# Agent attention with soft MoE: round weights in the selection matrices, denominators from slot sums, no filler products, a new order

## The chip, the cores and the metric

The kernel runs on one core of a Trainium2 chip. The core has TensorE (PE, matrix products into PSUM), VectorE (DVE), ScalarE (ACT), GpSimd (POOL) and SyncE (SP, which issues the large transfers); 16 DMA engines move data. The metric is the device time of one execution in microseconds; the median of several runs counts.

## The reference

Attention through 49 agents per batch, then a soft mixture of experts over all 4 x 11456 rows. All data is float32.

```python
B, N, C = 4, 11456, 128            # q, k, v; agents: (4, 49, 128)
def sm(a, b):                       # softmax(scale * a @ b^T)
    s = scale * (a @ b.transpose(0, 2, 1)); s = s - s.max(-1, keepdims=True)
    e = np.exp(s); return e / (e.sum(-1, keepdims=True) + 1e-09)
agent_v = sm(agents, k) @ v         # (B, 49, 128)
x = (sm(q, agents) @ agent_v).reshape(B * N, C)
# soft MoE: 8 experts, 4 slots each, so 32 slots; phi: (128, 32)
logits = x @ phi
d = np.exp(logits - logits.max(0)); d /= d.sum(0) + 1e-09     # over all rows, for each slot
slot_input = (d.T @ x).reshape(8, 4, 128)
slot_out[e] = np.maximum(slot_input[e] @ w1[e], 0) @ w2[e]    # F = 1024
c = np.exp(logits - logits.max(1)); c /= c.sum(1) + 1e-09     # over the slots, for each row
out = c @ slot_out
```

## The kernel before

The rows of a batch are laid out as four streams of 90 cells with 32 rows each. They are loaded in groups of 16 cells (1024 KB; the last groups of a batch are smaller): 24 K groups, 24 V groups and 25 q groups.

- A **K group**: `kx` and `kv` load it, `ks` makes the agent scores on PE, `km`, `kz`, `kb`, `kr` keep the running maximum, `ke` takes the exponential on ACT, `kT` transposes on DVE, `kE` (line 315, `ev`) multiplies with V on PE and `kA` adds to the batch's accumulator on DVE. After a batch's last group `kg` and `kh` make `agent_v` and `bd_m`, agents times `phi`.
- A **q group**: `qx` loads, `qs` scores, `qt` transposes on DVE so that a row's 49 scores lie side by side, `qm` takes the maximum. In the even groups (`DEN_ACT`) ACT takes the exponential with its sum (`qE`); in the odd ones POOL subtracts (`qu`), ACT takes the exponential (`qe`) and DVE sums 49 columns (`qd`, line 445). `qw`, `qr`, `qN` divide; `qp` and `qc` transpose on PE and copy on ACT.
- A **round** is two q groups (the last is the seventh group of batch 3 alone); there are 13. `ql` makes the slot logits on PE in PSUM (`lq`), `qM`, `r2`, `r4`, `r3` find each slot's maximum (`m_all`), `qv` transposes the logits into `x_all` on DVE, where they stay for the output. `r5` turns the maximum into a row (`mb`), `ru` subtracts it on POOL (line 546), `re` takes the exponential on ACT (line 551), and `rg` multiplies with the agent weights into `gp` (line 559); `rc` copies that to `g_all`. `cr`, `cu`, `ce` prepare the output's softmax in place in `x_all`.
- The **tail**: the rounds' maxima give each round a weight (`nm`, `wt`, `wr`, `ws`). The weights of the first nine rounds (batches 0 to 2) are made ahead (`ea` to `ei`), those of the last four at the end. POOL scales `g_all` by the weights (`ee`, `gl`), PE sums the rounds with the matrix `sel_st` (`ef`, `gm`, `l1`) and makes the slots' inputs `si` (`l3`, `l4`). `d0` to `d2` make the denominators from `g_all`'s last column. Then `mh` (`hp`, line 753), `mr` (relu, `hs`), `mt` (`htp`), `mc` (`ht`), `mo` (`so_p`, line 785) are the experts, `ms`, `sb`, `sd` spread and scale their outputs into `sob`. `fl` are filler products that nobody reads.
- The **output**, in 25 chunks of `x_all`: `os`, `oe`, `or`, `om` normalise, `ot` transposes on DVE, `oo` multiplies with `sob` on PE, `va` (DVE) and `vb` (ACT) copy PSUM to SBUF, `od` stores.

All steps stand in one list, `ORDER`, written out as a table of tokens. Every engine, and SP's queue of transfers, works through its own steps in that order, each waiting for its inputs; nothing overtakes. A buffer (`BUFS`) goes to the next taker in the list's order. w1 and w2 come in eight loads of 1024 KB: three of w2 take q buffers, the others take the room of the K and V buffers and so wait for the last K group (`ends`).

```python
FILL = (3, 2, 2, 2)
CHUNKS = [4, 4, 8] + [16] * 21 + [8]
    ends = [(f, i) + x for i in range(NK - 3, NK) for f, x in (
        ("ks", (1,)), ("ke", (1,)), ("kT", ()), ("kE", ()))]
```

Of the kernel before, what the change touches and what calls it, by code (L numbers as in the profile page):

```python
# [50 lines left out]
ORDER = """
qx5 wu qs5.0 qs5.1 qt5 qm5 qx0 qs0.0 qs0.1 qt0 qx3 qu5 qe5 qm0 qs3.0 qE0.0 qd5 qw5 qs3.1 qt3 qm3
qE0.1 qE0.2 qE0.3 qw0 qu3 qe3 qx2 qs2.0 qs2.1 qt2 qm2 qE2.0 kx0 ks0.0 ks0.1 qr5 km0 kz0 qd3 qx1
qs1.0 qs1.1 qx4 kb0 kr0 qE2.1 ke0.0 qN5 qs4.0 qs4.1 qr0 qt1 qw3 qN0 kp0 kx1 qm1 qt4 qr3 qm4 ks1.0
qE2.2 ks1.1 qp0.0 qp0.1 ke0.1 kT0 qN3 qE2.3 qE4.0 km1 kz1 qx6 qs6.0 qs6.1 kb1 kr1 qw2 qr2 qc0 qt6
qu1 qe1 kx2 ke1.0 ke1.1 qE4.1 ka1 ks2.0 ks2.1 qd1 km2 qN2 qp2.0 qp2.1 qx7 kT1 qw1 qr1 qN1 kp1 qc2
kz2 qE4.2 qE4.3 qs7.0 qs7.1 kx3 qt7 kv0 kb2 kr2 qp3.0 qp3.1 qc3 qw4 qm7 qu7 ke2.0 ke2.1 qm6 qE6.0
qr4 qx8 qN4 ks3.0 ks3.1 km3 ka2 kE0 qp1.0 kA0 kz3 qs8.0 qs8.1 kp2 kb3 qp1.1 kT2 qe7 qE6.1 qd7 kr3
qw7 qc1 qE6.2 qE6.3 qr7 ke3.0 qw6 kv1 kE1 kx5 ks5.0 ks5.1 qN7 kA1 qt8 qm8 ke3.1 kp3 ka3 kT3 kx4
qE8.0 qE8.1 ks4.0 qr6 ks4.1 km4 kz4 kv2 kE2 kb4 kr4 kp4 ke4.0 km5 ke4.1 kz5 kx6 ks6.0 ks6.1 kA2  # L60
qE8.2 kT4 kb5 kr5 qE8.3 ka4 ke5.0 qw8 qN6 ke5.1 kv3 kE3 km6 kz6 kb6 kr6 kT5 kv4 qr8 qN8 kE4 ke6.0
kA3 kA4 ka5 kv5 kE5 qx11 qs11.0 qs11.1 ke6.1 cx0 kA5 kg5.1 kT6 kg5.2 kh5.1 kg5.3 kh5.2 kh5.3 ql1
qt11 qm11 qx9 qp4.0 qM1 qv1 kh5.4 qu11 qe11 qd11 r21 qp4.1 qc4 qs9.0 qs9.1 qt9 ql0 qM0 r20 qw11
qr11 qN11 kx8 qp6.0 r41 qp6.1 qc6 kx7 ks7.0 r31 qv0 ks7.1 km7 qp5.0 r40 kp6 r30 qp5.1 kz7 qc5 r50
ru0.0 ks8.0 ks8.1 qm9 kb7 kr7 qx12 ke7.0 ke7.1 qs12.0 qs12.1 ql2 kp7 re0.0 rg0.0 km8 kz8 qt12
ru0.1 re0.1 r51 qm12 rg0.1 kb8 rc0 qx10 qs10.0 qM2 kr8 r22 qu9 qv2 ru1.0 ru1.1 qe9 qE12.0 ka8
qs10.1 qt10 qE12.1 kp8 kv6 r42 r32 kx9 qd9 kT7 kE6 kA6 ks9.0 ks9.1 km9 qm10 qp8.0 qp8.1 kz9 qE12.2
qE12.3 qw12 kv7 kE7 qr12 cr3 ke8.0 qN12 qc8 ke8.1 ka7 kA7 kT8 kb9 re1.0 kr9 qE10.0 re1.1 kp9 kx10
ks10.0 qw9 ke9.0 cr4 ks10.1 rg1.0 qx13 km10 qs13.0 qs13.1 ke9.1 kz10 rg1.1 kb10 kx11 ks11.0 ks11.1
kT9 qE10.1 qE10.2 kr10 rc1 ke10.0 kv8 kx12 qr9 kE8 qt13 qN9 km11 kz11 kp10 kb11 qm13 kr11 kA8 qu13  # L70
qz5 ke10.1 ka10 r52 ru2.1 ru2.0 qe13 ka11 re2.1 cu3 ks12.0 kT10 ks12.1 km12 kz12 ke11.0 ka9 ke11.1
kv9 kE9 cr0 kb12 kr12 kA9 cr1 cu1 kT11 qd13 qp7.0 kv10 kE10 qE10.3 ke12.0 qw10 qr10 cr2 kA10 kv11
ke12.1 kp12 qN10 kE11 qp7.1 qw13 qc7 kA11 kg11.1 kg11.2 kh11.2 kT12 qr13 cr5 qN13 cu2 qx15 qs15.0
qs15.1 qt15 re2.0 kh11.4 kh11.1 qm15 qu15 kg11.3 kh11.3 rg2.0 rg2.1 rc2 ql3 kx13 qM3 r23 qp10.0
qp10.1 qc10 qv3 qe15 qd15 ce2 ks13.0 ks13.1 km13 qw15 r43 r33 r53 qp11.0 qp11.1 kz13 qc11 qx14
# [955 lines left out]
```

## Time and profile before

| what | value |
|---|---|
| median of 3 runs | 293.61 us (293.21 to 293.80) |
| the profiled execution | 293.71 us, span 291.9 us |
| busy share of the span: PE, DVE, ACT, POOL | 85%, 76%, 68%, 44% |
| read from memory, written | 79.98 MB, 23.59 MB |
| end of the last K group's products (`kE`) | 189.0 us |
| start of the experts' first product (`hp`) | 215.6 us |
| issue of the first output transfer | 231.9 us |

The span runs from the first to the last instruction; the execution's own time is 1.8 us longer. The three times at the foot cut the span into the loads with their work, the tail and the output.

### The profile page before, as it was taken

The numbers are of one execution on the slowest core, as the hardware profiler recorded it, in microseconds if no ns is written. First come the engines' busy times: TensorE is split into PE (matmuls) and PEld (weight loads), VectorE is DVE, ScalarE is ACT, GpSimd is POOL, SyncE is SP. The second block draws the span as 40 slices with busy tenths as digits, with TensorE's granted clock in tenths as the row PEclk, the third lists the DMA queues.
The fourth block names the chain that finished last, engine by engine and source line by source line (L and its number), as shares of the span: only waits on it lengthen the run. The fifth ranks groups of instructions, "written<-read, shape, count | busy, mean of one in ns | idle before, by whom it ended". The sixth has DMA issues, their size and how long they took to land.

```text
span 291.9 us, 8505 instructions
## 1 busy us (share of the span) xinstructions
PE 249.5 (85%) x3382; PEld 134.1 (46%) x3382; DVE 222.3 (76%) x431; ACT 199.6 (68%) x678; POOL 128.9 (44%) x135
## 2 busy tenths in 40 slices
...
GB/s 276 384 423 419 419 422 356 417 420 418 423 320 355 425 419 337 416 371 392 419 391 382 423 390 352 96 360 424 368 7 0 44 408 424 413 421 423 412 422 274
DMA packets 16311, 104.12 MB, mean 357 GB/s; under 512 B 1936, under 2 KB 2192, under 8 KB 5008
## 3 DMA queue, kind: packets, MB, share of 16 engines
...
q14 instruction: 12, 0.10, 0.1%
HBM read 79.98 MB, written 23.59 MB: 355 GB/s over the span
## 4 chain that ended last, share of the span: by engine, by line
PE 53%; DMA 32%; DVE 5%; ACT 4%; issue 2%; SPq 1%; POOL 1%; ACTq 0%; DVEq 0%
DMA out<-ot 12%; PE sk L238 10%; PE ev L315 10%; PE sq L238 9%; PE tp L466 7%; DMA kt<-kT 7%; DMA vt<-vL 7%; DMA qt<-qT 6%; PE lq L514 4%; PE gp L559 3%; ACT ot L841 3%; PE fl L850 1%; PE so_p L785 1%; PE hp L753 1%; DVE ct L820 1%
## 5 line engine op out<-in xcount | busy, mean ns | idle before, releaser
L455 POOL TENSOR_TENSOR pt<-pt,rt 128x784 f32<-128x784 f32 (+3 forms) x20 | 27.1, 1356 | 55.9 <-DVE rt L451 37.6
L238 PE MATMUL sk<-kt,ag 128*32 128x512 f32 (+1 forms) x384 | 46.2, 570 | 3.4 <-DMA kt<-kT 2.6
L238 PE MATMUL sq<-qt,ag 128*32 128x512 f32 (+3 forms) x400 | 44.4, 562 | 4.8 <-DMA qt<-qT 4.8
L440 ACT ACTIVATE pt<-pt,mx 128x49 f32<-128x49 f32 x148 | 47.5, 325 | 0.0
L315 PE MATMUL ev<-vt,et 128*64 128x129 f32 x720 | 44.6, 275 | 2.9 <-DMA vt<-vL 1.8
L841 ACT COPY ot<-pb 128x1536 f32<-128x1536 f32 (+2 forms) x25 | 32.5, 1311 | 16.9 <-DMA out<-ot 12.3
L315 PEld LDWEIGHTS ev<-vt,et 128*64 128x64 f32 x720 | 39.4, 136 | 9.3 <-issue 3.4
L828 PE MATMUL pa<-ct,sob 32*128 32x512 f32 (+2 forms) x50 | 32.4, 759 | 11.8 <-DVE ct L820 9.3
L546 POOL TENSOR_TENSOR dt<-x_all,mb 128x512 f32<-128x512 f32 (+3 forms) x25 | 29.2, 1189 | 19.8 <-DVE mb L542 9.4
L298 ACT ACTIVATE es<-sk,nm 128x512 f32<-128x512 f32 (+1 forms) x48 | 30.0, 650 | 10.1 <-DVE nm L289 4.6
L828 PE MATMUL pb<-ct,sob 32*128 32x512 f32 (+2 forms) x150 | 33.1, 760 | 0.0
L814 POOL TENSOR_TENSOR x_all<-x_all,cd 128x512 f32<-128x512 f32 (+2 forms) x25 | 23.4, 963 | 20.2 <-DVE cd L809 20.2
L471 ACT COPY pT<-tp 128x1024 f32<-128x1024 f32 (+3 forms) x25 | 23.1, 923 | 10.1 <-PE tp L466 9.9
L838 DVE COPY ot<-pa 128x512 f32<-128x512 f32 (+2 forms) x25 | 15.4, 620 | 18.6 <-DMA out<-ot 15.7
L270 DVE TENSOR_REDUCE mt<-sk 128x2 f32<-128x1024 f32 (+1 forms) x24 | 27.7, 1154 | 2.3 <-PE sk L238 2.1
L308 DVE STREAM_TRANSPOSE et<-es 128x1024 f32<-128x1024 f32 (+1 forms) x24 | 28.0, 1165 | 0.5 <-ACT es L298 0.4
L440 ACT ACTIVATION_READ_ACCUMULATOR pt<-pt,mx 128x1 f32 x148 | 27.9, 188 | 0.0
L415 DVE STREAM_TRANSPOSE pt<-sq 128x1024 f32<-128x1024 f32 (+3 forms) x20 | 21.8, 1095 | 7.6 <-PE sq L238 7.4
L571 POOL TENSOR_TENSOR x_all<-x_all,r_all 128x512 f32<-128x512 f32 (+3 forms) x25 | 23.7, 968 | 4.9 <-DVE r_all L567 3.5
L828 PEld LDWEIGHTS pa<-ct,sob 32*128 32x128 f32 x50 | 9.7, 230 | 33.1 <-DVE ct L820 19.8
L238 PEld LDWEIGHTS sq<-qt,ag 128*32 128x32 f32 x400 | 11.2, 111 | 24.8 <-issue 19.6
L425 POOL TENSOR_TENSOR pt<-pt,mx 128x784 f32<-128x784 f32 (+2 forms) x10 | 12.9, 1290 | 20.0 <-DVE mx L420 15.4
(120 smaller groups left out, 433.5 us busy)
## 6 DMA issues: line engine op xcount, KB each, us to landing
...
vt<-vL SPq DMA_DIRECT2D x20, 1032.0 KB, 10.2
qt<-qT SPq DMA_DIRECT2D x20, 1024.0 KB, 10.0
...
```

The lines of the kernel that those rows point to most:

```text
L238: t_.matmul(sp[32 * q4:32 * q4 + 32, h, :nt], ag[:, b, 32 * h:32 * h + 32], xv[:, q4, :], start=True, stop=True)
L270: v_.tensor_reduce(out=k["mt"][:, 0:2], in_=k["s"][:, :, :nt], axis=AX.X, op=ALU.max, negate=True)
L298: s_.activation(out=k["e"][:, h, :nt], in_=k["s"][:, h, :nt], func=AF.Exp, bias=k["nm"][:, 2 * h:2 * h + 1])
L308: v_.transpose(out=k["et"][:, :n].rearrange("p t (h a) -> p h t a", h=2), in_=k["e"][:, :, :nt].rearrange("p h (t a) -> p h t a", a=32))
L315: t_.matmul(k["ev"][o:o + AW, :], k["et"][:, c, :], k["v"][:, c, :], start=c < 2, stop=c >= n - 2)
L440: s_.activation(out=x, in_=x, func=AF.Exp, bias=q["mx"][:, c:c + 1], accum_out=q["rt"][:, c:c + 1])
L455: g_.tensor_tensor(out=x, in0=x, op=ALU.mult, in1=q["rt"][:, :n].unsqueeze(2).to_broadcast([P, n, A]))
L546: g_.tensor_tensor(out=q["dt"][:, :q["n"]], in0=x_all[:, q["at"]:q["at"] + q["n"]], op=ALU.subtract, in1=r["mb"].unsqueeze(1).to_broadcast ...
L571: g_.tensor_tensor(out=x_all[:, x], in0=x_all[:, x], op=ALU.subtract, in1=r_all[:, x].unsqueeze(2).to_broadcast([P, q["n"], S]))
L814: g_.tensor_tensor(out=x, in0=x, op=ALU.mult, in1=z["cd", j].unsqueeze(2).to_broadcast([P, n, S]))
L828: t_.matmul(pb[:, r - 1, :32 * n] if r else pa[:, :32 * n], sob[32 * r:32 * r + 32, :], z["ct", j][32 * r:32 * r + 32, :32 * n], start=Tru ...
L841: s_.copy(out=o_ov(j)[:, 1:4], in_=z["pb", j][:, :, :32 * CHUNKS[j]])
```

## The change

- **Constants and first loads.** The five 128-column matrices after `CO_AB` are gone; `sel_st` and `sel_ts` are cut from `sel_d`, `sel_on` is set on the chip. The first load of the agents brings batch 0's alone, the others come with `cx` and are scaled in a new step `am`.
- **Folds.** In the q groups 5, 9, 13, 17, 21 POOL adds the two halves of 50 columns (`qf`), and DVE sums 25 columns.
- **Late rounds.** `m_all` holds the negative maximum. In the rounds 10, 11 and 12 ACT takes the exponential straight from PSUM with the maximum as its bias (`rx`), and DVE transposes that into `dt` (`ry`); `r5`, `ru` and `re` are gone there.
- **Round weights.** `ws` multiplies the weights into the selection matrix (`wse`), so that PE's sum scales; the steps `ee`, `gl` on POOL and `l0` on DVE are gone, and the last round is copied by `rc` as the others.
- **Denominators.** They come from the last row of the rounds' sums `gt` by small products (`dE`, `d1`, `d3`).
- **Experts.** `si` is written with a stride of 36 and read with one of 32, so that the eight experts' outputs land in the rows of their slots and add up in one PSUM tile: one `ms`, one `sb`. `sd` moves from ACT to DVE. `hp` of the first four experts comes first.
- **No `fl`; chunks** `[4, 4, 8, 8] + [16] * 21`; **all of `ORDER` is new**.

```diff
 ORDER = """
-qx5 wu qs5.0 qs5.1 qt5 qm5 qx0 qs0.0 qs0.1 qt0 qx3 qu5 qe5 qm0 qs3.0 qE0.0 qd5 qw5 qs3.1 qt3 qm3
+wu qx0 qs0.0 qs0.1 kx0 ks0.0 ks0.1 qt0 qm0 qx1 qs1.0 qE0.0 qE0.1 qE0.2 km0 qs1.1 qt1 qx5 qE0.3 qm1
...
-FILL = (3, 2, 2, 2)
+FILL = (0, 0, 0, 0)
+LATE_EXP = (10, 11, 12)
+FOLD = (5, 9, 13, 17, 21)
 WARM = 5
-CHUNKS = [4, 4, 8] + [16] * 21 + [8]
+CHUNKS = [4, 4, 8, 8] + [16] * 21
...
+        def qf():
+            q["fo"] = rp.tile([P, QC, A1 // 2], F32, name=f"fo_{i}", tag="fo", bufs=2)
+            g_.tensor_tensor(out=q["fo"][:, :n], in0=q["pt"][:, :n, 0:A1 // 2],
+                             in1=q["pt"][:, :n, A1 // 2:A1], op=ALU.add)
...
+        def rx():
+            r["dT"] = tile_("pt", [P, 2, QC, 32], f"dT_{ri}")
+            s_.activation(out=r["dT"][:, :, :n // 2], in_=r["lp"][:, :, :n // 2], func=AF.Exp,
+                          bias=m_all[:, ri:ri + 1])
+
+        def ry(q):
+            q["dt"] = tile_("dt", [P, QC, S], f"dt_{q['i']}")
+            c, m = q["c0"] // 2, q["n"] // 2
+            v_.transpose(out=q["dt"][:, :2 * m].rearrange("p (j e) s -> p e j s", e=2),
+                         in_=r["dT"][:, :, c:c + m])
...
     def z_ws(e):
-        lo, hi = (0, n0) if e else (n0, NR + 1)
-        v_.tensor_copy(out=wrs[:, lo:hi], in_=z["wr", e])
+        lo, hi = (0, n0) if e else (n0, NR)
+        sh = [P, hi - lo, S]
+        v_.tensor_tensor(out=wse[:, lo:hi], op=ALU.mult,
+                         in0=z["wr", e][:, :hi - lo].unsqueeze(2).to_broadcast(sh),
+                         in1=sel_st.unsqueeze(1).to_broadcast(sh))
...
-            t_.matmul(out_, g_all[:, ri, :], sel_st, start=ri == R0[b],
+            t_.matmul(out_, g_all[:, ri, :], wse[:, ri, :], start=ri == R0[b],
...
-    def gscale(lo, hi):
-        g_.tensor_tensor(out=g_all[:, lo:hi], in0=g_all[:, lo:hi], op=ALU.mult,
-                         in1=wrs[:, lo:hi].unsqueeze(2).to_broadcast([P, hi - lo, A1]))
+    def dsum(out_, bs):
+        for b in bs:
+            t_.matmul(out_, gt[:, b, :], ident[0:A1, A:A1], start=b == bs[0], stop=b == bs[-1])
...
-    def z_d0():
-        v_.tensor_reduce(out=gs1[:, 0:1], in_=g_all[:, n0:NR, A], axis=AX.X, op=ALU.add)
-        v_.scalar_tensor_tensor(out=gs1[:, 0:1], in0=gs1[:, 1:2], scalar=wrs[:, NR:NR + 1],
-                                in1=gs1[:, 0:1], op0=ALU.mult, op1=ALU.add)
```

**SP's queue, from batch 0's fourth K load to its last V load.** `kt`, `vt` and `qt` are loads of K, V and q. Ahead of these rows stand eight q and three K loads in before:

```order
L232 DMA kt_400<-kT 128x2048
L261 DMA vt_404<-vL 128x2064
L232 DMA qt_437<-qT 128x2048
L261 DMA vt_522<-vL 128x2064
L232 DMA kt_541<-kT 128x1280
L232 DMA kt_564<-kT 128x2048
L261 DMA vt_588<-vL 128x2064
L232 DMA kt_620<-kT 128x2048
L261 DMA vt_656<-vL 128x2064
L261 DMA vt_686<-vL 128x2064
L261 DMA vt_714<-vL 128x1290
```

and five q, four K and one V load in the change:

```order
L230 DMA qt_374<-qT 128x2048
L259 DMA vt_402<-vL 128x2064
L230 DMA kt_429<-kT 128x2048
L230 DMA kt_455<-kT 128x1280
L259 DMA vt_489<-vL 128x2064
L637 DMA cs<-cst 128x224
L638 DMA ph<-phi 128x32
L639 DMA ag<-agT 128x192
L259 DMA vt_521<-vL 128x2064
L230 DMA qt_567<-qT 128x2048
L259 DMA vt_586<-vL 128x2064
L259 DMA vt_605<-vL 128x1290
```

Two q loads (`qx7`, `qx8`) and batch 1's first K load (`kx6`) moved behind the last V load of batch 0; the constants moved ahead of it.

**DVE's queue, the end of round 11.** `t` and `m_all` are its maximum, `mb` the row made of it, `dt` and `dT` its exponentials, `cd` sums and reciprocals for the output, `r_all` row maxima. Before, from the last maximum to the last round's scaling `l0`:

```order
L538 TENSOR_REDUCE m_all<-t_2987 128x1
L657 TENSOR_REDUCE nmx<-m_all 32x1
L802 TENSOR_REDUCE cd_3007<-x_all 128x16
L525 STREAM_TRANSPOSE x_all<-lq_2903 128x2x11x32
L542 STREAM_TRANSPOSE mb_3051<-m_all 128x32
L802 TENSOR_REDUCE cd_3060<-x_all 128x16
L674 COPY wrs<-wr_3058 128x5
L567 TENSOR_REDUCE r_all<-x_all 128x16
L802 TENSOR_REDUCE cd_3085<-x_all 128x16
L809 RECIPROCAL cd_2753<-cd_2753 128x16
L719 TENSOR_SCALAR g_all<-gp_3066,wrs 128x50
```

In the change, from the last maximum to `l2`'s copy of the sums:

```order
L545 TENSOR_REDUCE m_all<-t_3020 128x1
L687 TENSOR_REDUCE nmx<-m_all 32x1
L838 TENSOR_REDUCE cd_3030<-x_all 128x16
L738 COPY de<-de_p 32x1
L565 STREAM_TRANSPOSE dt_3078<-dT_3036 128x2x8x32
L565 STREAM_TRANSPOSE dt_3080<-dT_3036 128x2x3x32
L845 RECIPROCAL cd_2816<-cd_2816 128x16
L704 TENSOR_TENSOR wse<-wr_3083,cs 128x128
L565 STREAM_TRANSPOSE dt_3111<-dT_3007 128x2x2x32
L532 STREAM_TRANSPOSE x_all<-lq_2843 128x2x16x32
L758 COPY gt<-gt_p 50x32
```

The transposes into `dt` and the product `wse` are new on DVE; the transpose of round 10's logits into `x_all` moved behind them.

**DVE's queue, from `si` to the second relu** (`hs`). Before:

```order
L733 TENSOR_TENSOR si<-si_p,sie 128x8x4
L567 TENSOR_REDUCE r_all<-x_all 128x6
L802 TENSOR_REDUCE cd_3170<-x_all 128x16
L567 TENSOR_REDUCE r_all<-x_all 128x16
L760 TENSOR_SCALAR hs_3177<-hp_3156 128x512
L567 TENSOR_REDUCE r_all<-x_all 128x16
L737 TENSOR_REDUCE gs_106<-g_all 128x1
L738 SCALAR_TENSOR_TENSOR gs_106<-gs_106,wrs 128x1
L760 TENSOR_SCALAR hs_3195<-hp_3180 128x512
```

In the change:

```order
L765 TENSOR_TENSOR si<-si_p,sie 128x8x4
L838 TENSOR_REDUCE cd_3141<-x_all 128x16
L532 STREAM_TRANSPOSE x_all<-lq_3009 128x2x11x32
L838 TENSOR_REDUCE cd_3147<-x_all 128x16
L797 TENSOR_SCALAR hs_3159<-hp_3150 128x512
L585 TENSOR_REDUCE r_all<-x_all 128x16
L797 TENSOR_SCALAR hs_3173<-hp_3164 128x512
```

The two steps on `gs` between the relus are gone, and round 11's transpose into `x_all` stands ahead of the first.

## Rows read from the trace of the kernel before

**Rows 1.** The page: busy time, granted clock, and rate of the DMA in 40 slices.

```profile
PE 249.5 (85%) x3382; PEld 134.1 (46%) x3382; DVE 222.3 (76%) x431; ACT 199.6 (68%) x678; POOL 128.9 (44%) x135
...
GB/s 276 384 423 419 419 422 356 417 420 418 423 320 355 425 419 337 416 371 392 419 391 382 423 390 352 96 360 424 368 7 0 44 408 424 413 421 423 412 422 274
```

**Rows 2.** Windows: stretch, length, busy us of each engine, clock, DMA share, GB/s.

```profile
0.00:10.00 10.00, 8.10 (x42) 4.21 (x42) 1.85 (x8) 1.70 (x2) 0.74 (x5) 1.00 0.80 310
10.00:31.00 21.00, 17.09 (x152) 5.66 (x152) 17.89 (x24) 17.70 (x85) 8.49 (x8) 1.00 1.01 411
31.00:70.00 39.00, 34.73 (x442) 19.92 (x434) 29.87 (x50) 28.00 (x123) 11.02 (x12) 1.00 1.00 407
70.00:189.00 119.00, 115.66 (x1945) 66.33 (x1944) 108.24 (x197) 96.10 (x374) 64.20 (x63) 1.00 0.94 373
189.00:203.20 14.20, 13.47 (x285) 9.60 (x284) 12.93 (x38) 11.06 (x27) 10.32 (x12) 1.00 0.90 370
203.20:215.50 12.30, 9.48 (x142) 6.61 (x139) 6.84 (x22) 4.56 (x15) 5.58 (x8) 0.58 0.63 259
215.50:231.90 16.40, 14.14 (x214) 8.82 (x215) 12.45 (x31) 7.33 (x23) 12.35 (x15) 0.90 0.01 2
231.90:245.00 13.10, 8.35 (x60) 2.76 (x55) 10.80 (x28) 9.43 (x14) 5.99 (x7) 0.92 0.95 386
245.00:291.90 46.90, 28.48 (x128) 10.24 (x120) 21.39 (x40) 23.77 (x21) 10.16 (x11) 0.68 0.96 396
```

**Rows 3.** The chain that ended last: start, length, engine and step, 184 to 229 us.

```profile
184.98 1.02 PE tp L466 x8
186.00 3.02 PE ev L315 x52
...
203.25 2.50 issue
...
215.57 3.57 PE hp L753 x16
...
222.25 2.00 PE htp L769 x16
...
224.91 3.75 PE so_p L785 x128
```

**Rows 4.** Timeline of PE, the start.

```profile
1.20 4.63 PE L618 MATMUL wu<-si 128*128 128x256 f32 x10 [1.20 <-DVE si L195]
```

**Rows 5.** Groups of instructions by shape: busy us, mean ns, idle before them.

```profile
L445 DVE TENSOR_REDUCE rt<-pt 128x16 f32<-128x784 f32 x6 | 5.7, 942 | 0.3 <-ACT pt L430 0.2
L445 DVE TENSOR_REDUCE rt<-pt 128x10 f32<-128x490 f32 x3 | 1.9, 639 | 0.0
L820 DVE STREAM_TRANSPOSE ct<-x_all 128x512 f32<-128x512 f32 x21 | 13.8, 681 | 0.3 <-POOL x_all L814 0.3
L298 ACT ACTIVATE es<-sk,nm 128x512 f32<-128x512 f32 x40 | 26.1, 677 | 8.3 <-DVE nm L289 4.6 <-DVE et L308 2.8 <-DVE rt L451 1.0
L551 ACT ACTIVATE dt<-dt 128x512 f32<-128x512 f32 x20 | 12.2, 626 | 0.7 <-POOL dt L546 0.5
L546 POOL TENSOR_TENSOR dt<-x_all,mb 128x512 f32<-128x512 f32 x20 | 25.7, 1300 | 16.1 <-DVE mb L542 9.4 <-PE sq L238 3.7 <-ACT pT L471 2.2
L546 POOL TENSOR_TENSOR dt<-x_all,mb 128x320 f32<-128x320 f32 x3 | 2.6, 881 | 0.1
```

**Rows 6.** Timeline of DVE, 220 to 224 us.

```profile
220.55 1.04 DVE L738 SCALAR_TENSOR_TENSOR gs<-gs,wrs 128x1 f32<-128x1 f32 x1
221.52 0.68 DVE L760 TENSOR_SCALAR hs<-hp 128x512 f32<-128x512 f32 x1
222.12 1.26 DVE L802 TENSOR_REDUCE cd<-x_all 128x16 f32<-128x512 f32 x2
```

**Rows 7.** SyncE: when it issues the first output, and a row of its waits.

```profile
231.87 4.42 SPq L845 DMA_DIRECT2D out<-ot  x5
...
SPq L261 <- PE ev L315: 12.4, 3, 7.6
```

More of the change, by code (lines that the diff above doesn't have):

```diff
@@ L56 @@
[L56 to L73, printed above, removed]
@@ L480, in q_ops @@
         x = o("qx", (), "D", qx, takes=("qt",))
-        s0 = o("qs", (0,), "P", lambda: qs_(0), deps=(x,), takes=("s",), gives=(("qt", x),))
+        s0 = o("qs", (0,), "P", lambda: qs_(0), deps=(x, ("am", 0)) if b else (x,), takes=("s",), gives=(("qt", x),))
         s1 = o("qs", (1,), "P", lambda: qs_(1), deps=(x, s0), gives=(("qt", x),))
@@ L592, in r_ops @@
         f = o("r3", (), "V", r3, deps=(f,), gives=(("a", qM_),))
-        mb = o("r5", (), "V", r5, deps=(f,))
+        late = ri in LATE_EXP
+        if late:
+            mb = o("rx", (), "A", rx, deps=(f, l0), takes=("pt",), gives=(("s", l0),))
+            ops[v]["deps"].append(mb)
+        else:
+            mb = o("r5", (), "V", r5, deps=(f,))
         g0 = None
@@ L606, in r_ops, with am @@
             g0 = g0 or f
-        if ri < NR - 1:
-            o("rc", (), "A", rc, deps=(f,), gives=(("a", g0),))
-        r["end"], r["g0"] = f, g0
+        r["end"] = o("rc", (), "A", rc, deps=(f,), gives=(("a", g0),))
     def cx():
-        nc.sync.dma_start(out=cs[:, CO_AB:], in_=cst[:, CO_AB:])
+        nc.sync.dma_start(out=cs[:, CO_1:], in_=cst[:, CO_1:])
         nc.sync.dma_start(out=ph, in_=phi)
+        nc.sync.dma_start(out=ag[:, 1:], in_=agT[:, 1:])
+    def am():
+        s_.mul(out=ag[:, 1:], in_=ag[:, 1:], mul=SCALE)
     def wu():
```

314 lines of the change are left out of this document (165 added, 149 removed).

## The prediction

> **What bounds the kernel now.** I read the page first [rows 1]. TensorE is busy 85% of the span, VectorE 76%, ScalarE 68%, so no engine is full over the whole; the question is which stretch is full of what. The table by stretches answers that [rows 2]. From 70 to 189 us TensorE is busy 115.7 of 119 us and VectorE 108.2: this stretch runs at the speed of these two, and the DMA engines (0.94) are close behind. From 10 to 70 us the DMA share is 1.00 and TensorE idles 3.9 + 4.3 us: there the loads set the pace. In the first 10 us 4.6 us of TensorE's work is `wu`, products that nobody reads [rows 4]. From 189.0, the end of the last K group's products [rows 3], to the first output transfer at 231.87 [rows 7] nothing is full: two queues of dependent steps decide, TensorE's and VectorE's. From then on the DMA share is 0.95 and 0.96: the output is written at the DMA's speed. So three lengths add up to the span of 291.9: 189.0 + 42.9 + 60.0. The profiled run itself took 293.71, 1.8 more than its span and 0.1 above the median of the three runs; I count from 293.7.
>
> In the middle length the chain [rows 3] shows four losses. At 203.25 TensorE stands for 2.50 us inside a group of products that has all its data ("issue": waiting for nothing that the profile shows). The granted clock is 0.58 of full from 203.2 to 215.5 [rows 2], the 1.2 GHz level for nearly all of that stretch. Sixteen of the `hp` products then take 3.57 us. And VectorE takes its second relu only at 221.52, after a reduce and the one-element `gs` step of 1.04 us [rows 6], so that the transposes start at 222.25.
>
> **The change, part by part.**
>
> *Length 1, up to the last K group's products.* The work of TensorE that stands ahead of them grows by one group of eight transposes (two groups taken in, one put off): +1.0 by the row of 1.02 us [rows 3]. The order of loads changes: ahead of batch 0's last V load the queue now has 7 q and 6 K loads where it had 9 and 7. That is 3 MB less, 0.2 MB of constants more, so about 2.9 MB at the 0.41 MB per us of that stretch [rows 2]: batch 0's summaries can begin some 7 us sooner, and with them the rounds' logits and products, the work that TensorE lacks between 31 and 70 us. I take 4 us of the 8.2 us idle there as won; bounds 0 and 8.2. The constants shrink by 270 KB, 0.65 us of DMA time, which is part of the same idle time and gives nothing of its own. The folds: five odd groups get an addition on GpSimd over 400 (250) columns, about 1.0 and 0.7 us by the rows of 512 and 320 columns [rows 5], and their sum on VectorE runs over half the columns: 0.94 falls to 0.55, 0.64 to 0.39 on the line through the two L445 rows. VectorE gains 1.7 us over the stretch, GpSimd pays 4.3. I set both at nothing: GpSimd is busy 64 of 119 us there [rows 2] and has room; if that cover is gone, each fold makes one q group's transposes late, at most 4.3 in all. Length 1: -3.0 (from -7.2 to +5.3).
>
> *Length 2, to the first output transfer.* Removed: GpSimd's two scalings of the sums, VectorE's scaling of the last one, the slot sums over `g_all` with the 1.04 us step [rows 6], nine filler pairs on TensorE, one of two evacuations of the expert sums. Added: `rx` and `ry` in the last three rounds for `r5`, `ru` and `re`. A 512-column piece paid 1.30 on GpSimd and 0.63 on ScalarE one after the other [rows 5]; now ScalarE reads PSUM once per round (between 0.68, the row of 512 columns, and twice that; I take 1.15 for 1024, 0.85 for 704) and VectorE transposes each piece in 0.68 [rows 5]. The link from a round's maximum to its products shrinks by about 1 us and leaves GpSimd, which the `cu` pieces fill. The slot weights are now multiplied into the selection matrix: 288 and 128 columns on VectorE where copies of 9 and 5 stood. No row shows that step; it lies between those copies (nearly nothing) and the 0.68 us of 512 columns; I take 0.42 and 0.29.
>
> So VectorE carries more of this stretch, and its list is the sum to make. Between its last accumulation and the first output copy stand 73 instructions; by the means of their groups (the 512-column ones 0.63 to 0.68, the 1024-column ones twice that) they sum to 32.8 us. Two in a row take less than their two durations (1.26 for two of 0.66, [rows 6]), so back to back they need about 28. In before, VectorE was busy 31 of 42 us here: about 11 us of waiting. The new order keeps some of it: `ry` of round 11 waits for `rx` behind seven ScalarE instructions, `si` for the sum's four products, `sob` for `d3` and `sb`. It drops the wait on GpSimd's scaling and puts `mr0.0` and `mr1.0` one instruction apart. I take 5 to 6 us of waiting: 33.5, plus 2 for a clock that falls for part of it (next paragraph) and 0.9 from the first copy to the transfer: 36.4 against 42.9, so -6.5. With 3 us of waiting and no fall it is 31.9, with the 11 us of before and half the price of a fall through 43.4: from -11 to +0.5. The weights don't bind: one of eight w loads now goes ahead of the last V loads, and the seven others, 7.3 MB at 0.41 MB per us, take 18 us from the last K group's end, while `si` on VectorE's list comes after 19 us.
>
> *The clock, weighed.* The row: with fillers, the clock still fell, at the 2.50 us pause, and was back before 222 [rows 2, 3]. Without fillers TensorE has about 15 us of work in the 21 us before `hp` (13.5 + 9.5 busy in before [rows 2], less 5 of fillers and some 3 that the half clock added), so a fall is as likely as not. At 2.4 GHz all of `hp` takes 3.6, the transposes 2.0, `so_p` 3.75 [rows 3]: 9.3 us, hidden beside the 11.7 us on VectorE's list between `si` and the copy of the expert sums. At 1.2 GHz they take twice as long, 18.6, and 6.9 us come out of cover. A fall that ends during `hp`, as in before, costs up to 2; I put in 2. The Trainium skill (TensorE: Matmul & The Clock Gate, Why this matters for your kernels) speaks against this part of the change: it asks for no idle gaps between bursts of matmuls, since a gap brings back the half clock. By that rule alone the whole 6.9 us would stand in the sum, 5 more than mine: the first rival below.
>
> *Length 3, the output.* More is left to do after the first output product: 5 row sums and 3 row maxima on VectorE, 5 subtractions on GpSimd, 5 exponentials on ScalarE. By [rows 6] that is 8 x 0.6 = 4.6 us of VectorE, and in 231.9 to 245 it had only 2.3 us to spare while the DMA already lost a little (386 GB/s [rows 2] against 408 to 424 in the page's slices of the output [rows 1]). The fourth output chunk is halved to 512 KB and the last one doubled, which leaves the bytes as they are. I take +1.7 (from 0 to 4.6).
>
> Sum: 293.7 - 3.0 - 6.5 + 1.7 = 285.9, told as **286.0**.
>
> **The rivals.**
> *The clock stays at the half level from the last round into `so_p`.* For: [rows 2] show 0.58 even with fillers. Against: `hp` and the transposes are continuous work, and in before the clock returned during `hp`. 286 + 5 = 291.
> *Everything overlaps: TensorE loses only 3 us before 70 us and VectorE waits 2 us in length 2.* For: nothing in the data forbids it, down to the 18 us of the weights. Against: [rows 2] show no stretch without waits. 281.5.
> *Loads held in the queue; slower.* SyncE issues in order, so a load that stands ahead of its buffer's release holds all behind it. The row of L261 shows one such wait of 7.6 us [rows 7], covered in before by loads on the way. In the new order a w load that needs a q buffer stands ahead of the last two V loads, and in the first 50 us K loads with two buffers stand close together. If two waits of that size meet no cover, TensorE idles in the full stretch: 286 + 10 = 296. It decides from 7.7 us of added idle on.
> *The gain is given back at the output.* Length 2 falls by 6.5 but TensorE's last K group is no sooner (+1.0) and VectorE's 4.6 us and GpSimd's five pieces all delay transfers: 293.7 + 1 - 6.5 + 5.5 = 293.7, no change.
>
> **How the numbers follow.** Forecast 0.55 (own range 283.5 to 289), clock 0.17, all overlaps 0.10, loads held 0.12, given back 0.06. 0.2% of this kernel is 0.6 us, about what its measurement can tell from no change. Faster: 0.55 + 0.17 + 0.10, less the edge of the clock case: 0.80. Same 0.06, slower 0.14 (the rest of the clock case with the held loads). The range reaches down to the overlap case and up past the clock case: 281.5 to 293.0 leaves out the held loads, the case without change and half of the overlap case, about 0.2.
>
> **What the new profile would show.** Right: the last `ev` of the last K group ends near 186; `hp` starts 21 to 23 us after it; the first output transfer near 222.5; GpSimd has no step between the last `rc` and the sums; DMA share above 0.9 from there to the end. Wrong: idle time of TensorE over 8 us between 70 us and the last `ev`, with waits on loads; a granted clock of half through `so_p`; output transfers waiting on `cd` or `ct` for more than 3 us in all; VectorE waiting over 8 us between the last `acc` and the first `ot`.

## The result and the profile after

The changed kernel takes 286.47 us (median of 4 runs, 285.01 to 287.29) where the kernel before took 293.41 beside it (4 runs): the ratio is 0.974, with a 95% interval from 0.970 to 0.978. The profiled run took 286.32 with a span of 284.3; it is read against the profiled run of before, 293.71 and 291.9. A few executions of a kernel are over 1.5% slower than its fastest; the ratios leave them out and the medians do not, and three of the six of e12_best, the profiled one among them, are such.

The page of after. The shares of 40 slices stand in tenths:

```profile
PE 243.7 (86%) x3370; PEld 130.6 (46%) x3370; DVE 221.3 (78%) x431; ACT 198.6 (70%) x678; POOL 126.2 (44%) x139
...
PEclk9999999999999999999999999999759797668555
DMA  7999999999999999999999999379700299999996
...
q8 instruction: 26, 0.43, 0.6%
```

A slice is 7.1 us. The granted clock dips in the 29th and 30th (199 to 213 us, and again in the output), and the DMA engines stand from 206 to 220, between the last weights and the first output. Queue 8 loads instructions, 26 times 16 KB, and comes up below.

The windows of after, with the columns of [rows 2]; the last two rows are a second cut of the stretch of the sums and the expert products:

```profile
10.00:31.00 21.00, 16.47 (x174) 6.34 (x169) 16.44 (x22) 16.58 (x77) 6.20 (x6) 1.00 1.01 419
31.00:70.00 39.00, 36.87 (x453) 19.57 (x447) 30.20 (x52) 25.07 (x106) 12.79 (x13) 1.00 1.02 414
70.00:184.95 114.95, 113.24 (x1931) 66.13 (x1924) 106.28 (x199) 98.31 (x395) 63.65 (x66) 1.00 0.96 389
184.95:199.40 14.45, 12.55 (x274) 8.71 (x273) 12.74 (x35) 11.98 (x32) 11.30 (x16) 1.00 0.92 369
199.40:207.80 8.40, 5.08 (x142) 4.20 (x142) 4.42 (x14) 4.83 (x13) 4.19 (x6) 0.68 0.60 246
207.80:223.00 15.20, 13.57 (x197) 7.79 (x198) 12.16 (x29) 4.06 (x14) 4.74 (x6) 0.84 0.01 2
223.00:236.00 13.00, 10.32 (x64) 3.98 (x63) 12.14 (x30) 11.37 (x20) 9.24 (x11) 0.87 0.84 338
...
202.40:212.60 10.20, 7.75 (x65) 3.44 (x57) 5.30 (x11) 3.24 (x8) 1.41 (x2) 0.50 0.19 76
212.60:222.90 10.30, 8.67 (x177) 6.54 (x170) 9.04 (x25) 3.56 (x13) 4.64 (x6) 1.00 0.01 2
```

TensorE's timeline of after: start, length, line and step, and in brackets the wait ahead of it and what ended it.

```profile
49.49 3.09 PE L313 MATMUL ev<-vt,et 128*64 128x129 f32 x52 [0.21 <-DMA vt<-vL]
...
181.87 3.09 PE L313 MATMUL ev<-vt,et 128*64 128x129 f32 x52
...
200.36 0.91 PE L577 MATMUL gp<-pt,dt 128*32 128x50 f32 x64
...
203.23 0.90 PE L710 MATMUL gt_p<-wse,g_all 128*50 128x32 f32 x8
206.30 0.63 PE L745 MATMUL fb<-fd,sel_on 32*128 32x32 f32 x2 [2.17 <-issue]
...
207.77 6.05 PE L790 MATMUL hp<-w1s,si 128*32 128x512 f32 x32
```

And the same for VectorE, then one row of GpSimd and the issue of the first output transfer by SyncE:

```profile
206.97 0.19 DVE L748 TENSOR_TENSOR sie<-sie,fb 128x32 f32<-128x32 f32 x1 [2.42 <-PE fb L745]
...
217.69 1.25 DVE L585 TENSOR_REDUCE r_all<-x_all 128x16 f32<-128x512 f32 x2
...
220.55 0.24 DVE L827 COPY so<-so_p 128x128 f32<-128x128 f32 x1
...
219.02 1.05 POOL L589 TENSOR_TENSOR x_all<-x_all,r_all 128x512 f32<-128x512 f32 x1 [3.51 <-DVE r_all L585]
...
223.01 20.49 SPq L881 DMA_DIRECT2D out<-ot  x12
```

The three lengths of the prediction can be read off. The products of the last K group end at 184.95 (181.87 and 3.09, less what the pipeline lets the next step overlap; the chain has 181.93 and 3.02) instead of 189.0: -4.1. From there to the first output transfer it is 38.1 us instead of 42.9: -4.8. From that to the end of the span it is 61.3 instead of 60.0: +1.2. The sum, -7.6, is the difference of the spans.

### The profile page after: what moved, and what is told of

The parts are those of the page before. It is cut to its first block, busy times and chain, and to the rows that moved or that the text cites. A ratio compares the mean times of both kernels' runs of the same rounds, so it can differ in the third digit from the quotient of the medians.

```text
span 284.3 us, 8467 instructions
## 1 busy us (share of the span) xinstructions
PE 243.7 (86%) x3370; PEld 130.6 (46%) x3370; DVE 221.3 (78%) x431; ACT 198.6 (70%) x678; POOL 126.2 (44%) x139
## 4 chain that ended last, share of the span: by engine, by line
PE 52%; DMA 28%; DVE 8%; ACT 4%; issue 3%; SPq 1%; ACTq 1%; DVEq 0%
PE ev L313 12%; PE sq L236 12%; DMA qt<-qT 10%; DMA out<-ot 10%; PE sk L236 9%; PE tp L470 6%; DMA vt<-vL 4%; DMA kt<-kT 3%; ACT ot L877 3%; PE gp L577 3%; PE lq L520 3%; PE pa L864 2%; PE hp L790 2%; DVE ct L856 1%; DVE cd L838 1%
## 5 line engine op out<-in xcount | busy, mean ns | idle before, releaser
L236 PE MATMUL sq<-qt,ag 128*32 128x512 f32 (+3 forms) x400 | 43.8, 554 | 3.8 <-DMA qt<-qT 3.6
L864 PE MATMUL pa<-ct,sob 32*128 32x512 f32 (+2 forms) x50 | 35.0, 824 | 11.5 <-DVE ct L856 8.0
L864 PE MATMUL pb<-ct,sob 32*128 32x512 f32 (+2 forms) x150 | 36.1, 834 | 0.0
L553 POOL TENSOR_TENSOR dt<-x_all,mb 128x512 f32<-128x512 f32 (+1 forms) x20 | 24.2, 1217 | 21.5 <-DVE mb L549 17.7
L413 DVE STREAM_TRANSPOSE pt<-sq 128x1024 f32<-128x1024 f32 (+3 forms) x20 | 21.9, 1097 | 2.0 <-PE sq L236 1.5
L236 PEld LDWEIGHTS sq<-qt,ag 128*32 128x32 f32 x400 | 10.9, 109 | 23.4 <-issue 16.7
L470 PE MATMUL tp<-cs,pt 128*128 128x128 f32 x140 | 21.3, 283 | 0.0
```

The costliest lines, as they stand in the source:

```text
L236: t_.matmul(sp[32 * q4:32 * q4 + 32, h, :nt], ag[:, b, 32 * h:32 * h + 32], xv[:, q4, :], start=True, stop=True)
L470: t_.transpose(q["tp"][:, h, j % 4, :], q["pt"][:, 2 * j:2 * j + 2, :].rearrange("p c a -> p (c a)"), ident)
L553: g_.tensor_tensor(out=q["dt"][:, :q["n"]], in0=x_all[:, q["at"]:q["at"] + q["n"]], op=ALU.add, in1=r["mb"].unsqueeze(1).to_broadcast([P, ...
L864: t_.matmul(pb[:, r - 1, :32 * n] if r else pa[:, :32 * n], sob[32 * r:32 * r + 32, :], z["ct", j][32 * r:32 * r + 32, :32 * n], start=Tru ...
```

## The experiments

Each kernel was timed against the kernel before on the same chip. The ratio is the figure to compare, since the median of before moved between 293.4 and 294.1 from one set to the next. The three lengths come from one profiled run each: end of the last K group's products, way from there to the first output transfer, and output. The profiled run of after lies 0.2 us below its median, but those of e2_tail, e7_shift32, e9_shift and e11_nofold lie 1.8, 3.5, 3.0 and 2.4 us below theirs, so small differences between the lengths of two kernels mean nothing.

| kernel | median, us | ratio to before, 95% | K products end | to first output | output |
|---|---|---|---|---|---|
| before | 293.41 | 1 | 189.0 | 42.9 | 60.0 |
| after | 286.47 | 0.974 (0.970 to 0.978) | 184.9 | 38.1 | 61.3 |
| e1_head | 294.87 | 1.005 (1.002 to 1.008) | 185.6 | 47.4 | 60.6 |
| e2_tail | 290.91 | 0.988 (0.983 to 0.994) | 189.2 | 36.9 | 60.9 |
| e3_opening | 290.72 | 0.991 (0.987 to 0.995) | 188.9 | 37.6 | 61.5 |
| e4_fill | 292.70 | 0.997 (0.994 to 0.999) | 185.6 | 44.3 | 61.5 |
| e5_nofill | 291.47 | 0.990 (0.987 to 0.994) | 188.8 | 39.7 | 60.1 |
| e6_nolate | 293.11 | 0.998 (0.995 to 1.001) | 185.1 | 44.6 | 61.8 |
| e7_shift32 | 298.74 | 1.013 (1.006 to 1.019) | 195.8 | 35.7 | 61.9 |
| e8_shift54 | 303.80 | 1.033 (1.028 to 1.038) | 205.8 | 35.9 | 61.9 |
| e9_shift | 287.72 | 0.981 (0.976 to 0.986) | 185.2 | 35.8 | 61.9 |
| e10_dve | 292.82 | 0.996 (0.993 to 1.000) | 186.8 | 35.6 | 67.7 |
| e11_nofold | 287.23 | 0.978 (0.974 to 0.983) | 185.5 | 35.8 | 61.7 |
| e12_best | 288.01 | 0.973 (0.965 to 0.980) | 191.1 | 35.3 | 62.5 |

### Where the first length was won

**The new head on the old kernel.** The tokens of ORDER up to kE23 (the last K group's products) are those of after, without its own am0 and qf; those of before follow.

```diff
-qx5 wu qs5.0 qs5.1 qt5 qm5 qx0 qs0.0 qs0.1 qt0 qx3 qu5 qe5 qm0
+wu qx0 qs0.0 qs0.1 kx0 ks0.0 ks0.1 qt0 qm0 qx1 qs1.0 qE0.0 qE0.1
 ...
```

> The kernel before, with the changed kernel's order up to the last K group's products and its own order, sums and fillers behind them; no folds, its own constants. Theory: the 4.1 us of the first length come from the order of loads and of the work on them. Then the last K group's products end near 185 instead of 189, and the whole takes about 289.4 (ratio 0.986). Rival A: the folds and the smaller constants give it; then the products end at 189 and the time stays near 293.4. Rival B: work was only moved past the products' end (the products of q group 18, two moved chunks of maxima); then they end near 185 but the first output transfer is at 231 as before, and the time is above 292.

TensorE's timeline and then ScalarE's:

```profile
182.54 3.09 PE L315 MATMUL ev<-vt,et 128*64 128x129 f32 x52
...
191.54 0.63 PE L351 MATMUL m<-ph,avt 128*128 128x32 f32 x2 [3.24 <-ACT avt L337]
...
186.84 3.07 ACT L576 ACTIVATE x_all<-x_all 128x512 f32<-128x512 f32 x6 [0.58 <-POOL x_all L571]
...
191.24 0.25 ACT L337 COPY avt<-avtp 128x128 f32<-128x128 f32 x1
```

Rival B held. The products end at 185.6, 3.4 us sooner and without folds or new constants, but the way to the output is 4.5 us longer: TensorE waits 3.24 us for a copy on ScalarE that stands behind six exponentials of chunks. The head alone gains nothing; the tail must fit it.

**The old head on the new kernel**, and **the old opening alone** (tokens up to kE5, batch 0's last K group). The edits are the reverse of the one above, with cx0 ahead of qx6 and each qf behind its qe.

> The changed kernel, folds and constants included, with the old order up to the last K group's products (each fold right behind its exponential, the constants' second part ahead of batch 1's first q load). Theory: the first length is as before, near 189, the way from there to the first output transfer stays near 38 and the output near 61: about 290 (3.5 us better than before). Rival A (folds and constants give the first length): near 185 and 286.5. Rival B (the tail is sooner only because the head left less work to it): the way to the first transfer is over 41, and the time is above 292.

> The changed kernel with the old order up to batch 0's last accumulation alone, its own order from there. Theory: what batch 0's last V load gained by going 3 MB sooner is what TensorE won, so nearly all of the 4 us are lost: the last K group's products end at 188 to 189, and the time is about 290. Rival: the order between 50 and 185 us won it; then they end near 185 and the time is 286.5 to 287.

TensorE's timeline of e3_opening:

```profile
57.15 3.09 PE L313 MATMUL ev<-vt,et 128*64 128x129 f32 x52 [0.32 <-DVE nm L287]
...
185.78 3.09 PE L313 MATMUL ev<-vt,et 128*64 128x129 f32 x52
```

Windows of e2_tail, and then a row of its chain:

```profile
208.00:213.35 5.35, 5.06 (x137) 4.40 (x135) 3.97 (x13) 2.84 (x9) 0.96 (x2) 0.71 0.12 44
213.35:226.10 12.75, 11.12 (x197) 7.40 (x198) 12.12 (x29) 4.17 (x15) 4.68 (x6) 1.00 0.01 1
```

```profile
213.35 3.69 PE hp L790 x32
```

The theory held in both. With the old opening batch 0's last K group is multiplied at 57.15 as in before (56.90), not at 49.49, and nearly the whole 4 us are gone at the end, 188.9, although everything behind these products stands in the new order. The opening was put back as a whole; its loads and the work on them were not tried apart. In e2_tail the length to the first output, 36.9, does not need the new head; and here `hp` ran at full clock, 3.69 us where after took 6.05.

**No folds** (`FOLD = ()`, qf tokens dropped).

```diff
-FOLD = (5, 9, 13, 17, 21)
+FOLD = ()
```

> The changed kernel without the five folds: VectorE sums whole q groups again, GpSimd adds nothing. Theory: both engines have room in the stretch to 185 us, so the last K group's products end within 0.5 us of 184.95 and the time is 286 to 287. Rival: VectorE is a limit there; 1.7 us more of it make the first length 1 to 2 us longer, 287.5 to 288.5. Rival 2: the folds make q groups late; without them the first length is 1 us shorter, 285.5.

From TensorE's timeline:

```profile
205.80 0.40 PE L745 MATMUL fb<-fd,sel_on 32*128 32x32 f32 x2 [2.08 <-issue]
```

The products end at 185.5, and the intervals of the two ratios overlap: no effect of the folds shows, though the intervals leave room for one of up to 3 us. The row is used below.

### Where the second length was won

**Fillers back into the changed kernel**, seven pairs where TensorE waits and two behind the expert sums. A pair is two full products here and two transposes in before, so that it shows as four records here (36 in all) and as two there (18): these fillers are twice those of before.

```diff
-FILL = (0, 0, 0, 0)
+FILL = (3, 2, 2, 2)
...
-... ql11 or2 ... dE ej ... wr ws ... gm qv10 ... d1 qv11 ... sb sd
+... ql11 fl0 or2 ... dE fl1 ej ... wr fl2 ws ... gm fl3 fl4 qv10 ... d1 fl5 fl6 qv11 ... sb fl7 fl8 sd
```

> The changed kernel with nine filler pairs on TensorE again, put where it waits between 197 and 208 us, and two behind the expert sums as before. Theory: TensorE's waits and its pause at 204 let the clock fall, and fillers of 0.5 us each cannot bridge a pause of 2 us that no data causes, so the hp products still begin at half clock, and the fillers on the chain cost 0.5 to 2: 287 to 288.5. Rival: the fillers hold the clock at 2.4 GHz; then the 32 hp products take about 3.6 us instead of 6.1 and the time is near 285.

TensorE's timeline, and then the chain:

```profile
208.23 2.50 PE L887 MATMUL fl<-cs 128*128 128x128 f32 x8
...
212.44 2.50 PE L887 MATMUL fl<-cs 128*128 128x128 f32 x8
```

```profile
214.94 5.21 PE hp L791 x32
```

**No fillers in the kernel before.**

```diff
-FILL = (3, 2, 2, 2)
+FILL = (0, 0, 0, 0)
```

> The kernel before without its nine filler pairs on TensorE, nothing else changed. Theory now, after the run with fillers added: the pairs are no cover but part of the chain. Seven of them stand between 208.1 and 215.5 in the profile of before and take 0.69 to 0.73 each, 4.3 us, and VectorE, ScalarE and the sums wait behind them. Then the way from the last K group's products to hp falls from 26.5 to 23 or less, and the time is 289 to 290.5, most of what the second length gained. Rival (the sum as predicted): VectorE's list sets that length and the pairs lie beside it; then the time is 293 to 294. Rival 2: without fillers the clock stays at half through the expert products; then 5 us come on top, 295 or more.

TensorE's timeline:

```profile
205.23 0.92 PE L558 MATMUL gp<-pt,dt 128*32 128x50 f32 x62 [2.21 <-issue]
...
208.35 1.22 PE L558 MATMUL gp<-pt,dt 128*32 128x50 f32 x44 [1.08 <-ACT dt L550]
```

In e4_fill the pairs take 0.7 to 1.25 us each, most of them on the chain, and the way to the first output grows by 6.3. The direction was as expected; the price is over three times the highest that was expected. The fillers do not hold the clock: `hp` takes 5.21, as in before with fillers (5.3, from 215.50 to 220.81), where the full clock gives 3.69. Dropping them from before shortens its way by 3.2 us (42.9 to 39.7) and its time by 2.9 (0.990). That lies between the theory and its rival: `hp` starts 23.7 us after the last K group's products, and 23 or less was expected. So fillers were a cost, and two thirds of the second length's gain can be had by dropping them.

**The last three rounds in the old form** (`LATE_EXP = ()`): maximum, subtraction on GpSimd, exponential on ScalarE.

```diff
-LATE_EXP = (10, 11, 12)
+LATE_EXP = ()
...
-... rx10 ry10.0 ... ry10.1 ... rx11 ... ry11.0 ry11.1
+... r510 qv10 ru10.0 re10.0 ... ru10.1 re10.1 ... r511 qv11 ... ru11.0 re11.0 ru11.1 re11.1
```

Round 12 changes in the same way.

> The changed kernel with the last three rounds in the old form: the maximum transposed, subtracted on GpSimd, one exponential a piece on ScalarE, the transpose of the logits ahead of them. Theory: the link from maximum to products is about 1 us longer in each of the two rounds that the sums wait for, and 1.2 us of transposes go ahead of it on VectorE's list, so hp starts 2 to 4 us later: 288.5 to 290. Rival: the form of these rounds costs nothing since the queue of instructions on TensorE sets the pace; 286 to 287.

TensorE's timeline:

```profile
196.80 0.56 PE L578 MATMUL gp<-pt,dt 128*32 128x50 f32 x32 [1.75 <-ACT dt L570]
...
201.94 0.90 PE L578 MATMUL gp<-pt,dt 128*32 128x50 f32 x32 [2.49 <-ACT dt L570]
...
209.97 1.22 PE L578 MATMUL gp<-pt,dt 128*32 128x50 f32 x44 [1.29 <-ACT dt L570]
211.89 0.40 PE L578 MATMUL gp<-pt,dt 128*32 128x50 f32 x8 [0.71 <-ACT dt L570]
```

The theory's direction held, its size was too small: 6.5 us, as much as nearly all of the change's gain. TensorE waits 6.2 us in these four rows for the exponentials of a round's pieces. The new order was made for the new form, and the old one was not given an order of its own, so the 6.5 us are the price of the old form in this order. They do not add up with the fillers' price.

### The pause that no data explains

Between `gt_p` and `fb` TensorE stands for 2.16 us in after (2.17 in the row above), and a 16 KB instruction load (queue 8) falls right ahead of it, at 203.81 us. The transfers from 203.7 to 204.2 us:

```profile
q1 hardware_dynamic: 21, 0.11, 51.9%
q8 instruction: 1, 0.02, 12.8%
```

Three kernels shift that load with tiny products behind the warm-up `wu`: 32 and 54 with weights of 128 columns, then 32 with weights of 4.

```diff
+        for _ in range(32):
+            t_.matmul(w[:, 0:4], ident, ident[:, 0:4], start=True, stop=True)
...
+        for _ in range(32):
+            t_.matmul(w[0:4, 0:4], si[:, 0, 0:4], si[:, 0, 0:4], start=True, stop=True)
```

> The changed kernel with 32 further tiny products of 4 columns behind the warm-up products in the first 5 us, which nobody reads. They only shift the place in TensorE's instruction stream at which its 16 KB instruction loads fall, by about half a load's period. Theory: the pause of 2.16 us at 204.14 is TensorE waiting for instructions, because the rounds' products of the last stretch use up a load's worth in under 3 us; then the pause moves to another place in the stretch 197 to 209 or goes, and the time changes by up to 2 us either way (284.5 to 288). Rival: the pause belongs to the step (the product of the one-column scale), and stays in front of it; 286.5, unchanged.

> As the run before, with 54 tiny products instead of 32, which puts the instruction load of 203.8 some 216 instructions earlier, near 199, where TensorE waits for VectorE anyway, and the next one near hp, whose products are long. Theory: no pause of over 1 us between 199.5 and 207.8 that no data causes, hp 1.5 to 2 us sooner, 284.5 to 285.5. Rival: pause unchanged ahead of the same product, 286.5.

> The changed kernel with 32 products of 4 by 4 elements (weights of 4 columns, not of 128 as in the two runs before) behind the warm-up products, which nobody reads. Theory: they shift the instruction loads as the 32 wide ones did and cost little: the pause of 2.16 us is gone, the way from the last K group's products to the first output transfer is 35.7 to 36 us instead of 38.1, the first length stays within 0.5 us of 184.95, and the time is 284 to 285. Rival A: the pause was gone in those runs because everything ran 10 us later against the loads of weights; then it is back and the time is 286.5. Rival B: such a product costs as much as a wide one (0.34 us); then the first length grows by 10 us again, 296.

TensorE's timeline of e7_shift32 (one row) and of e9_shift:

```profile
5.45 10.73 PE L650 MATMUL wu<-cs 128*128 128x4 f32 x64
```

```profile
5.57 1.72 PE L650 MATMUL wu<-si 128*4 128x4 f32 x63
...
200.04 1.95 PE L577 MATMUL gp<-pt,dt 128*32 128x50 f32 x64
...
204.09 0.90 PE L712 MATMUL gt_p<-wse,g_all 128*50 128x32 f32 x8
204.92 0.63 PE L747 MATMUL fb<-fd,sel_on 32*128 32x32 f32 x2
...
206.40 5.45 PE L792 MATMUL hp<-w1s,si 128*32 128x512 f32 x32
```

All three lose the pause at this step (in e9_shift `fb` begins 0.83 us after `gt_p`, in after 3.07), and their way to the first output is 35.7 to 35.9 us. The times of the first two lie far above what was expected. The wide products make the first length 10.9 and 20.8 us longer (their rows take 10.73 us in e7_shift32 and 19.93 in e8_shift54), and the clock has a part in that: up to 8.50 us, at full clock, 28 of them take 3.05 us, 0.11 each, and from 11 to 14 us, at 0.50, 15 take 3.00, 0.20 each. A narrow one takes 0.027, at full clock. In e9_shift the lengths came as expected; the 284 to 285 us hold for the profiled run (284.74) and not for the median.

But the pause was moved and not removed. The two kernels of the next section contain the same 32 narrow products, and there TensorE pauses for 1.08 us (e10_dve) and 0.75 (e12_best) inside the `gp` products. TensorE's timeline of e12_best:

```profile
205.79 0.96 PE L577 MATMUL gp<-pt,dt 128*32 128x50 f32 x63
207.51 0.29 PE L577 MATMUL gp<-pt,dt 128*32 128x50 f32 x1 [0.75 <-issue]
```

The place can be counted. When TensorE pauses it has begun 2983 to 2985 product records since the start in after, e3_opening, e11_nofold, e10_dve and e12_best alike, whichever step that is, and 2854 or 2855 in before, e1_head and e5_nofill, 256 instructions of its trace earlier (weight loads count too). In all eight it goes on 2.3 to 2.5 us after a load on queue 8 began (in after 203.81 and 206.30). Where there is no pause, TensorE comes to that place no sooner than this: 2.3 to 2.6 us after the load's start in e4_fill, e7_shift32, e8_shift54 and e9_shift, whose 64 `gp` products ran at half clock or near it (1.56 to 1.95 us for 0.91), 3.4 and 6.3 us after it in e2_tail and e6_nolate. So the pause goes with the place in the instruction stream and not with the step. Its length is what is left of some 2.4 us when the work that TensorE still has is done. Why these loads begin so late is open.

What the pause is worth in time is not shown: e9_shift stands at 0.981 (0.976 to 0.986), not below after. Its 64 `gp` products ran at half clock (1.95 us for 0.91), and e11_nofold had the pause (2.08, e3_opening 1.92), a better clock behind it (`fb` 0.40 for 0.63), and also came to 35.8. One profiled run of a kernel tells this length to 1 or 2 us only.

### What the output waits for

**VectorE's list around the expert sums.** In after VectorE copies the sums (`so`) at 220.55, 1 us after TensorE has them, behind the two maxima of 217.69 and more. Both kernels here contain the narrow products. First two maxima (`cr19`, `cr22`) and two sums (`os11`, `os14`) go behind the first output copies; then, in the last run, the maxima `cr18` and `cr19` and the sum `os14` go ahead, to where VectorE waits for `hp`, and `cr22` and `os11` behind the scaling `sd`.

Most tokens of other engines are left out; `cu` and `om` are GpSimd's.

```diff
-... d2 cr18 cr19 or4 os14 ot1 or5 ot2 ot3 ms cu19 os11 om7 ... sd cr22 va0 os10 os12 va1 ...
+... d2 cr18 or4 ot1 or5 ot2 ms ot3 om7 ... sd va0 os11 os10 os12 va1 cr22 cr19 cu19 va2 os14 ...
...
-... os9 mr0.0 cr21 mr1.0 ... cu8 om1 om0 ... cr18 cr19 os14 ... cu19 om7 ... cu18 om4
+... os9 cr18 cr19 mr0.0 cr21 os14 mr1.0 ... cu8 om7 cu18 cu19 om1 om0 ... om5 om4
```

> As the run before, with VectorE's list around the expert sums reordered: two chunk maxima and two row sums that no early output chunk needs go behind the first output copies, so that the copy of the expert sums and the scaling behind it follow TensorE at once. Theory: the two waits of TensorE (0.97 and 0.52 us) go, the first output transfer leaves 1.0 to 1.5 us sooner, and since the output needs the moved steps only later, the time is 0.7 to 1.3 below the run before: 283 to 284. Rival: VectorE's 2.5 us come back as waits of the output, and the time equals the run before.

> The changed kernel with the 32 small products of 4 by 4, and VectorE's and GpSimd's lists reordered once more: the two chunk maxima and one row sum that stood before the copy of the expert sums now stand where VectorE waits for the hp products, so that GpSimd's two subtractions and one scaling behind them also come ahead of the output; another row sum and one maximum go behind the scaling of the expert sums. Theory: in the run with VectorE's list reordered the output lost 6 us because a subtraction on GpSimd waited for the late maximum, and the scalings of the output chunks stood behind it in GpSimd's queue. With the maxima early the output takes 60 to 61 us instead of 67.7, the way from the last K group's products to the first transfer is 34.5 to 35.5, and the profiled run takes 282 to 283.5, below all runs before. Rival: VectorE has no room ahead of the expert sums at all; its relus come late, the way to the first transfer is 36.5 to 37.5 and the time equals the run with the small products alone (about 285 for its profiled run).

SyncE, GpSimd and TensorE in e10_dve:

```profile
222.41 21.08 SPq L883 DMA_DIRECT2D out<-ot  x10
...
225.31 1.05 POOL L589 TENSOR_TENSOR x_all<-x_all,r_all 128x512 f32<-128x512 f32 x1 [8.52 <-DVE r_all L585]
...
230.18 1.22 PE L866 MATMUL pa<-ct,sob 32*128 32x512 f32 x1 [4.84 <-DVE ct L858]
```

GpSimd in e12_best:

```profile
222.60 2.05 POOL L852 TENSOR_TENSOR x_all<-x_all,cd 128x512 f32<-128x512 f32 x2 [2.84 <-DVE cd L847]
229.29 1.05 POOL L852 TENSOR_TENSOR x_all<-x_all,cd 128x512 f32<-128x512 f32 x1 [4.64 <-DVE cd L847]
```

In e10_dve it came worse than the theory and its rival: the first transfer left 0.2 us sooner on its way, the output took 5.8 us longer than in e9_shift, and the median is 5.1 us above that of e9_shift. The row of GpSimd shows the cause: its queue goes in order, cu19 waited for the late cr19 until 225.31, and behind it stood the scalings that the chunks' transposes need. With cr19 early the output is back at 62.5. That run's profiled execution (290.7) had already lost 6 us ahead of the last K group's products, so only its later lengths are read, and the 282 to 283.5 us expected of it were missed; the lowest of its six times is 284.02. Its way to the first output, 35.3, is the shortest in the table, by less than one profile can tell, but GpSimd still waits 4.64 us, now for a reciprocal on VectorE, and the ratio 0.973 (0.965 to 0.980) cannot be told from that of after. No run here beat the changed kernel by what its measurement can tell.

## Why the prediction was right, and where not

**The sum.** 286.0 was forecast, 286.47 came. The three terms were -3.0, -6.5 and +1.7, and measured -4.1, -4.8 and +1.2. The first and the third came out 1.1 and 0.5 better, the second 1.7 worse. The errors cancel, so that a sum within 0.5 us is luck; the directions and the order of the sizes are not. Two sums of the working are slightly off and change nothing: 8 x 0.6 us of VectorE's added work is 4.8 and not 4.6, and the case in which everything overlaps comes to about 281.2 by its terms and not to 281.5.

**Length 1.** The mechanism was right: batch 0's last products start at 49.49 and not at 56.90, 7.4 us sooner (forecast: some 7), and e3_opening shows that the opening carries the whole term. The size came out higher since I looked for the gain only between 10 and 70 us. By the windows TensorE's idle time falls by 1.5 us there (8.2 to 6.7) and by 1.6 more from 70 us to the end of the products (3.3 to 1.7), and of my +1.0 for the added transposes nothing shows (its busy time up to there falls from 175.6 to 174.1). The folds at nothing: no run speaks against it (e11_nofold).

**Length 2** is the term that was mis-sized, by 1.7 us. For VectorE's list from its last accumulation to the first output copy I had 28 busy, 5 to 6 of waiting and 2 for the clock, 35.5 in all. In that stretch (185.35 to 222.37 us) it was busy 28.3 and waited 8.7, 37.0 in all. So the busy time was right, and the waiting 1.2 us more than the two terms for it. Of the 8.7, 2.42 is the wait for `fb` behind TensorE's pause. The chain of before had shown such a pause of 2.50 [rows 3], I listed it among the losses, and then no term said that it stays. That this is the missing part is argued and not shown: the three shifted kernels needed 35.7 to 35.9 where I had 36.4, but so did e11_nofold, which has the pause (35.8). The fillers' own price was missing too: I took them for something beside VectorE's list, but without them before is 2.9 us faster (e5_nofill). And "shrinks by about 1 us" for the link of a round was far too little in this order (e6_nolate: 6.5 us in all). The products of the weights with the selection matrix, for which no row stood, took 0.45 and 0.23 us where I had 0.42 and 0.29.

**The signs.** `hp` started 22.8 us after the last K group's products and the first transfer left at 223.0, as said. But one sign of being wrong came: between its last accumulation and its first transpose for the output VectorE waited 8.5 us (21.9 busy of 30.4), over the limit of 8. And the DMA share stayed below 0.9 at the start of the output.

**The clock.** It fell, from 202.4 to 212.6 at 0.50, and was back for the transposes and `so_p`. My 2 us for a fall that ends during `hp` is near what rows show (6.05 for 3.69, 2.4 us). But I tied its chance to the missing fillers, and that was wrong: with them, before and e4_fill ran `hp` at half clock for the most part too (5.30 and 5.21 us). The Trainium skill (TensorE: Matmul & The Clock Gate, Why this matters for your kernels) warns against idle gaps between bursts; the trace agrees that the fall follows a stretch with gaps (TensorE was busy 2.42 of the 5.00 us from 197.4 to 202.4). Filling gaps with products that nobody reads cost 3.2 us of the way in before and 6.3 in e4_fill, and the clock fell there too.

**Length 3.** Right in kind: DMA share 0.84 in the first 13 us of the output where before had 0.95, with GpSimd and VectorE late; +1.2 for +1.7. GpSimd's queue stood behind cu19 (3.51 us of waiting until 219.02), and e10_dve shows what such a wait can cost the output. That it was the cause in after is not shown: in e12_best cu19 came early and the output took 62.5 us, no less than in after (61.3).

**The rivals.** Half clock through `so_p`: no, it ended at 212.6. Loads held in the queue: no, TensorE idles 1.7 us between 70 us and the last `ev`. Given back at the output: only the 1.2 of the third term. Everything overlaps: no, for the pause and for 8.7 us of VectorE's waits.

Not settled: what the pause is worth in time, and what made the output 1.2 us longer. The constants' size, the selection matrices, the denominators and the experts' common PSUM tile were not tried alone.
